# Where cache units lie in SBUF, how they are cut into loads, and a PSUM bank for the last output group, in a decode kernel that streams 282 MB

## The chip, the cores and the metric

One core of one Trainium2 chip. The metric is the device time of one execution in microseconds (us), as the median of several runs.

## The reference, cut to what matters

Four tokens (B = 4) go through a layer norm, then through an attention over a cache and through a small gated MLP, and the two results are added to the input.

```python
q = (xn @ wq).reshape(4, 1, 32, 128).transpose(0, 2, 1, 3)      # wq 640 x 4096
scores = einsum('bhqd,bhkd->bhqk', q, k_cache) * 128 ** -0.5     # k_cache 4 x 32 x 4096 x 128
p = softmax(scores)
o = einsum('bhqk,bhkd->bhqd', p, v_cache)                        # v_cache 4 x 32 x 4096 x 128
attention = o.transpose(0, 2, 1, 3).reshape(4, 1, 4096) @ wo     # wo 4096 x 640
# beside it: z = gelu(xn @ w_in), layer norm of one half, gate, @ w_out
return x + attention + mlp
```

All is bf16. K and V together are 268 MB, and each byte is used once. So this is a kernel that streams.

## The kernel before: the parts concerned

The heads are taken in 4 groups of 8, and a *unit* is one batch entry of one group: 128 partitions x 64 KB = 8.4 MB. There are 16 K units and 16 V units. The kernel's buffer in SBUF (the on-chip memory that loads land in) has five slots of half a unit, so a unit lies in two neighbouring slots.

```python
SL = T * Dh // 2                          # half a unit: 32 KB a partition
kv = const.tile([P, 5 * SL], BF16)        # five slots
# order of the loads, all on one queue: K0 K1 K2 K3 V0 K4 V1 K5 ... V11 K15 V12 V13 V14 V15
place = {("k", 0): 3, ("k", 1): 0, ("k", 2): 2, ("k", 3): 0}     # first of the two slots
for u in range(B, NU):
    place[("k", u)] = 1 if u % 2 == 0 else 0
for u in range(NU):
    place[("v", u)] = 3
place[("v", NU - 3)] = 1
place[("v", NU - 1)] = 0
# where a unit's load is cut (in tokens); a unit without an entry is one transfer
cuts = {("k", u): (0, T // 2, T) for u in range(NU) if u < B or u % B == B - 1}
cuts[("v", NU - 1)] = (0, 128, 192, 240, T)
first = {u: u % 2 for u in range(B, NU) if ("k", u) not in cuts}  # the half transposed first
```

wq lies in slots 0 and 1 at the start, w_in and w_out in slot 2. For each K unit VectorE makes 8 transposes (in blocks of 32 x 32, each element an f32 that holds two bf16), and TensorE multiplies each with the query. After four K units comes the softmax of the group, then the V units of the group are multiplied. A load waits until the last reader of its slots is done.

```python
nc.vector.transpose(kT[...], kw)                     # 8 of these per K unit
nc.tensor.matmul(S_ps[32 * q:32 * q + 32, e], ...)   # 8 per transpose
...
for w in range(NW):                                  # V: 64 matmuls, tokens in order
    nc.tensor.matmul(O_ps[32 * q:32 * q + 32], lhsT=Zb[b % 2][:, w], rhs=vv[:, w * 4 * Dh:(w + 1) * 4 * Dh], ...)
```

The tail: the output projection of all groups, the MLP and the residual collect in one bank of PSUM (the memory that TensorE's results go to), even rows of wo in partitions 0 to 63, odd ones in 64 to 127, and the halves are added at the end. The last group of wo loads in four pieces.

```python
emit_proj(NG - 1, range(0, HG // 2))
nc.vector.tensor_copy(out=o_1[:], in_=proj[64:128, 0:NO2])
emit_proj(NG - 1, range(HG // 2, HG))                 # all in partitions 0 to 63
nc.vector.tensor_tensor(out=o_bf[:], in0=proj[0:64, 0:NO2], in1=o_1[:], op=ALU.add)
# o_bf goes out on two queues
```

## Time and profile before

| what | before |
|---|---|
| median of the runs | 666.28 us, later 666.24 with 6 runs |
| span of the profiled run | 664.3 us |
| bytes read | 282.25 MB, 425 GB/s over the span |
| share of the load queue's packets in 16 engines' span | 98.7% |
| VectorE, TensorE busy | 54%, 45% |
| from the landing of the last wo piece (660.31) to the issue of the output (661.83) | 1.53 us |

In a timeline line the columns are start, length, engine, line of the kernel, operation, and in brackets the idle time ahead and what ended it. In a window line they are the window, its length, busy time and count of PE, PEld, DVE, ACT and POOL, then granted clock (of TensorE, as a share of full speed), DMA share and GB/s. The share books a packet's whole time at its start, so with packets of 2.4 us a window of 2 us can read above 1.

### The profile page before, as it was taken

What the parts mean: (1) busy time and instruction counts of PE and PEld (TensorE: products, weight loads), DVE (VectorE), ACT (ScalarE), POOL (GpSimd) and SP (SyncE); (2) the same over time, 40 slices, a digit from 0 to 9 for tenths busy, and PEclk for the clock granted to TensorE, in tenths of its full rate; (3) what the DMA queues carried; (4) which work ended last, traced back from release to release, by engine and by line L of the source; (5) the groups of instructions that cost most, each with busy time, mean ns of one, the idle gap of its engine ahead of it and who ended that gap; (6) DMA issues with size and microseconds to landing.
All of it is one profiled execution on the core that took longest, in us unless ns stands there. A gap on an engine that the chain in (4) does not pass through costs nothing.

```text
span 664.3 us, 5584 instructions
## 1 busy us (share of the span) xinstructions
PE 300.6 (45%) x2366; PEld 110.9 (17%) x2366; DVE 359.9 (54%) x340; ACT 82.6 (12%) x169; POOL 6.2 (1%) x24
## 2 busy tenths in 40 slices
PE   0566656336072556225436075533507154623154
PEld 0321212112021122001112022111202012211021
DVE  5388997456190849509155286745528084940002
ACT  0300000710100000530200000070100000062200
POOL 0000000000000000000000000000000000000000
PEclk9767876568576587677758576766957768767785
DMA  8999999999999999999999999999999999999995
GB/s 370 427 440 427 424 439 438 439 438 435 435 418 439 427 417 460 422 439 426 423 442 439 430 412 451 434 426 442 431 426 427 434 439 416 461 435 407 425 416 238
DMA packets 7669, 282.61 MB, mean 425 GB/s; under 512 B 872, under 2 KB 1244, under 8 KB 1756
## 3 DMA queue, kind: packets, MB, share of 16 engines
q1 hardware_dynamic: 7628, 282.25, 98.7%
q8 instruction: 18, 0.29, 0.2%
q14 instruction: 7, 0.06, 0.0%
q10 hardware_dynamic: 16, 0.01, 0.0%
HBM read 282.25 MB, written 0.01 MB: 425 GB/s over the span
## 4 chain that ended last, share of the span: by engine, by line
DMA 75%; issue 10%; DVE 10%; PE 3%; ACT 1%; SPq 0%; DVEq 0%; ACTq 0%
DMA kv<-in_A_k_cache_dram 64%; DVE kT L352 9%; DMA kv<-in_A_v_cache_dram 5%; DMA kv<-in_A_wo_dram 3%; DMA kv<-in_A_wq_dram 2%; PE O L434 2%; PE q L247 1%; DVE xd L417 0%; DVE kv L255 0%; ACT Zb L398 0%; PE proj L475 0%; ACT kv L255 0%; ACT p L406 0%; PE misc L278 0%; DVE pT L410 0%
## 5 line engine op out<-in xcount | busy, mean ns | idle before, releaser
L352 DVE STREAM_TRANSPOSE kT<-kv 128x2048 f32<-128x2048 f32 x128 | 283.4, 2277 | 127.4 <-DMA kv<-in_A_k_cache_dram 127.4
L363 PE MATMUL S<-kT,QZ 128*32 128x512 bf16 x1024 | 197.8, 522 | 227.1 <-DVE kT L352 227.1
L363 PEld LDWEIGHTS <-QZ 128*32 128x32 bf16 x1024 | 62.5, 114 | 356.8 <-issue 340.1
L434 PE MATMUL O<-kv,Zb 128*32 128x512 bf16 x1024 | 72.5, 444 | 61.3 <-ACT Zb L398 30.2
L441 DVE TENSOR_SCALAR R<-O,Mk 128x128 f32<-128x128 f32 x16 | 5.6, 351 | 126.4 <-PE O L434 126.4
L398 ACT ACTIVATE Zb<-xd,MkE 32x256 bf16<-32x256 bf16 x112 | 51.4, 498 | 111.7 <-PE O L434 110.3
L406 ACT ACTIVATE p<-S,negmax 128x512 bf16<-128x512 f32 x8 | 5.4, 683 | 395.1 <-DVE negmax L384 395.1
L434 PEld LDWEIGHTS <-Zb 128*32 128x32 bf16 x1024 | 31.9, 109 | 100.8 <-issue 54.5
L451 PE MATMUL misc<-R,SelR 128*32 128x128 f32 x32 | 6.6, 290 | 26.0 <-DVE R L443 26.0
L417 ACT COPY xd<-pT 32x256 bf16<-32x256 bf16 x28 | 17.2, 613 | 5.7 <-DVE pT L410 5.2
L443 DVE SCALAR_TENSOR_TENSOR R<-O,Mk,R 128x128 f32<-128x128 f32 x48 | 16.9, 351 | 1.7
L417 DVE COPY xd<-pT 32x256 bf16<-32x256 bf16 x36 | 13.1, 364 | 0.6
L339 POOL COPY QZ<-q 32x32 bf16<-32x32 bf16 x16 | 5.1, 320 | 422.6 <-PE S L363 395.3
L410 DVE STREAM_TRANSPOSE pT<-p 128x1024 bf16<-128x1024 bf16 x4 | 5.0, 1245 | 6.3 <-ACT p L406 6.3
L370 DVE TENSOR_REDUCE m<-S 128x2 f32<-128x1024 f32 x4 | 4.9, 1224 | 6.4 <-PE S L363 6.4
L451 PEld LDWEIGHTS misc<-R,SelR 128*32 128x32 f32 x32 | 2.3, 109 | 33.6 <-DVE R L443 24.8
L255 DVE CAST kv<-q 128x512 bf16<-128x512 f32 x4 | 2.5, 682 | 9.8 <-PE q L247 9.8
L475 PE MATMUL proj<-kv,oT 128*4 128x320 bf16 x64 | 6.3, 430 | 2.4 <-DMA kv<-in_A_wo_dram 1.8
L247 PE MATMUL q<-kv,xnT 128*32 128x512 bf16 x40 | 4.5, 629 | 5.5 <-DMA kv<-in_A_wq_dram 5.5
L454 DVE SCALAR_TENSOR_TENSOR om<-misc,rinv,MkH 32x1024 bf16<-32x1024 f32 x4 | 5.1, 1272 | 2.2 <-PE misc L451 2.2
L422 PE MATMUL misc<-rowsum,SelPe 128*32 128x1 f32 x16 | 2.1, 202 | 9.0 <-ACT p L406 9.0
L375 PE MATMUL misc<-dg,ones_f 128*128 128x256 f32 x8 | 2.7, 416 | 7.6 <-DVE dg L372 7.6
(94 smaller groups left out, 62.4 us busy)
## 6 DMA issues: line engine op xcount, KB each, us to landing
kv<-in_A_k_cache_dram SPq DMA_DIRECT2D x14, 4096.0 KB, 34.7
kv<-in_A_wq_dram SPq DMA_DIRECT2D x1, 5120.0 KB
kv<-in_A_v_cache_dram SPq DMA_DIRECT2D x1, 4096.0 KB, 40.2
kv<-in_A_wo_dram SPq DMA_DIRECT2D x3, 1280.0 KB, 19.2
kv<-in_B_w_in_dram SPq DMA_DIRECT2D x1, 2160.0 KB
kv<-in_A_v_cache_dram SPq DMA_DIRECT2D x1, 2048.0 KB
kv<-in_A_v_cache_dram SPq DMA_DIRECT2D x1, 1536.0 KB
kv<-in_B_w_out_dram SPq DMA_DIRECT2D x1, 960.0 KB, 22.6
```

The lines of the kernel that those rows point to most:

```text
L247: nc.tensor.matmul(q4_ps[32 * j:32 * j + 32, hf * 512:hf * 512 + 512], lhsT=xnT[:, c, :], rhs=wq[:, c, n0:n0 + 512], start=(c == 0), stop= ...
L339: nc.gpsimd.tensor_copy(out=QZ[r0:r0 + 32, :, :, :, 8 + 8 * hp], in_=q3[r0:r0 + 32, :, NE * hp:NE * hp + NE, g * B:g * B + B].rearrange("p ...
L352: nc.vector.transpose(kT[:].rearrange("p (t r) -> p t r", r=32), kw)
L363: nc.tensor.matmul(S_ps[32 * q:32 * q + 32, e], lhsT=QZ[:, b, 2 * kh + w, e, w0:w0 + 32], rhs=kb[:, i, :, e, :, w], start=(b == 0 and k < ...
L398: nc.scalar.activation(out=dst, in_=src, func=ACT.Copy, scale=mk)
L406: nc.scalar.activation(out=p_bf[:, :, e, :], in_=S_ps[:, e], func=ACT.Exp, bias=negmax[:, e:e + 1], scale=scale, accum_out=rowsum[:, e:e + 1])
L417: op(out=xd[32 * hp:32 * hp + 32, :, q, :], in_=pT[32 * q:32 * q + 32, :, hp, :].rearrange("p t x -> p x t"))
L434: nc.tensor.matmul(O_ps[32 * q:32 * q + 32, :, :], lhsT=Zb[b % 2][:, w].rearrange("p h c -> p (h c)"), rhs=vv[:, w * 4 * Dh:(w + 1) * 4 * ...
L441: nc.vector.tensor_scalar(out=R, in0=O_ps[:, 0, :], scalar1=Mk4[:, 0:1], scalar2=None, op0=ALU.mult)
L443: nc.vector.scalar_tensor_tensor(out=R, in0=O_ps[:, c, :], scalar=Mk4[:, c:c + 1], in1=R, op0=ALU.mult, op1=ALU.add)
L451: nc.tensor.matmul(oh[:], lhsT=SelR[:, b].rearrange("p h b -> p (h b)"), rhs=state["R"][:, b, :], start=(b == 0), stop=(b == B - 1))
L475: nc.tensor.matmul(proj[r0:r0 + B, 0:NO2], lhsT=oT[:, c, :], rhs=wo_t[g][:, c, hf * NO2:(hf + 1) * NO2], start=False, stop=(g == NG - 1 an ...
```

## The change

The intent: with the slots dealt the other way round, K0 to K2 can each load as one transfer without V0 waiting for all of K2; K3 lies in slots 4 and 0, which are not neighbours, and keeps its two halves. V15 loads in two pieces and not four. The last wo group gets a PSUM bank of its own, so that its matmuls need not wait until the old bank is read.

```diff
-    place = {("k", 0): 3, ("k", 1): 0, ("k", 2): 2, ("k", 3): 0}
+    place = {("k", 0): (3, 4), ("k", 1): (0, 1), ("k", 2): (2, 3), ("k", 3): (4, 0)}
     for u in range(B, NU):
-        place[("k", u)] = 1 if u % 2 == 0 else 0
+        place[("k", u)] = (3, 4) if u % 2 == 0 else (2, 3)
     for u in range(NU):
-        place[("v", u)] = 3
-    place[("v", NU - 3)] = 1
-    place[("v", NU - 1)] = 0
-    cuts = {("k", u): (0, T // 2, T) for u in range(NU) if u < B or u % B == B - 1}
-    cuts[("v", NU - 1)] = (0, 128, 192, 240, T)
+        place[("v", u)] = (0, 1)
+    place[("v", 0)] = (1, 2)
+    place[("v", NU - 3)] = (2, 3)
+    place[("v", NU - 1)] = (3, 4)
+    cuts = {("k", u): (0, T // 2, T) for u in range(NU) if u % B == B - 1}
+    cuts[("v", NU - 1)] = (0, 192, T)
 ... (cut: addressing of a unit by its two slots; wo groups in slots 4, 0, 1, 2 and not 2, 4, 3, 2)
-                nc.sync.dma_start(out=x_res[0:32:4, :], in_=x_flat.rearrange("b (h n) -> (b h) n", h=NH))
+                for r0, r1 in ((0, 3), (3, 2 * B)):
+                    nc.sync.dma_start(out=x_res[4 * r0:4 * r1:4, :], in_=x_rows[r0:r1])
 ...
-    emit_proj(NG - 1, range(0, HG // 2))
-    nc.vector.tensor_copy(out=o_1[:], in_=proj[64:128, 0:NO2])
-    emit_proj(NG - 1, range(HG // 2, HG))
+    nc.vector.tensor_copy(out=o_1[:], in_=proj[0:64, 0:NO2])
+    nc.vector.tensor_tensor(out=o_1[:], in0=proj[64:128, 0:NO2], in1=o_1[:], op=ALU.add)
+    last = ps_l.tile([64, NO2], F32)
+    for c in range(HG):                    # c == 0 starts the bank, with 32 columns
+        for hf in range(NH):
+            nc.tensor.matmul(last[32 * hf:...], lhsT=..., rhs=wo_t[NG - 1][:, c, hf * NO2:(hf + 1) * NO2],
+                             start=(c == 0), stop=(c == HG - 1))
-    nc.vector.tensor_tensor(out=o_bf[:], in0=proj[0:64, 0:NO2], in1=o_1[:], op=ALU.add)
+    nc.vector.tensor_tensor(out=o_bf[:], in0=last[:], in1=o_1[:], op=ALU.add)
```

More of the change, by code (lines that the diff above doesn't have):

```diff
@@ L72 @@
     ps_j = ctx.enter_context(tc.tile_pool(name="ps_j", bufs=1, space=bass.MemoryType.PSUM))
+    ps_l = ctx.enter_context(tc.tile_pool(name="ps_l", bufs=1, space=bass.MemoryType.PSUM))
     misc_ctr = [0]
@@ L120, with unit @@
             seq.append(("k", u + B))
-    place = {("k", 0): 3, ("k", 1): 0, ("k", 2): 2, ("k", 3): 0}
+    place = {("k", 0): (3, 4), ("k", 1): (0, 1), ("k", 2): (2, 3), ("k", 3): (4, 0)}
     for u in range(B, NU):
-        place[("k", u)] = 1 if u % 2 == 0 else 0
+        place[("k", u)] = (3, 4) if u % 2 == 0 else (2, 3)
     for u in range(NU):
-        place[("v", u)] = 3
-    place[("v", NU - 3)] = 1
-    place[("v", NU - 1)] = 0
-    cuts = {("k", u): (0, T // 2, T) for u in range(NU) if u < B or u % B == B - 1}
-    cuts[("v", NU - 1)] = (0, 128, 192, 240, T)
-    first = {u: u % 2 for u in range(B, NU) if ("k", u) not in cuts}
-    def unit(item):
-        return at_slot(place[item], 2 * SL)
+        place[("v", u)] = (0, 1)
[4 more added lines that the diff above has]
+    cuts[("v", NU - 1)] = (0, 192, T)
+    first = {u: u % 2 for u in range(B, NU) if ("k", u) not in cuts}
+    def unit(item, t0, t1):
+        s0, s1 = place[item]
+        assert s1 == s0 + 1 or t1 <= T // 2 or t0 >= T // 2
+        if t0 >= T // 2:
+            return at_slot(s1, (t1 - t0) * Dh, t0 * Dh - SL)
+        return at_slot(s0, (t1 - t0) * Dh, t0 * Dh)
     def load_unit(item):
@@ L138, in load_unit @@
         cache = A_k_cache if key == "k" else A_v_cache
-        dst = unit(item)
         src = cache[b, g * HG:(g + 1) * HG].rearrange("e (m t) d -> (e m) (t d)", t=T)
@@ L142, in load_unit @@
         for t0, t1 in zip(c[:-1], c[1:]):
-            nc.sync.dma_start(out=dst[:, t0 * Dh:t1 * Dh], in_=src[:, t0 * Dh:t1 * Dh])
+            nc.sync.dma_start(out=unit(item, t0, t1), in_=src[:, t0 * Dh:t1 * Dh])
     wo_q = A_wo.rearrange("(g p c) n -> g p c n", p=P, c=HG)
-    wo_t = [at_slot((2, 4, 3, 2)[g], HG * NOUT).rearrange("p (c n) -> p c n", c=HG) for g in range(NG)]
+    wo_t = [at_slot((4, 0, 1, 2)[g], HG * NOUT).rearrange("p (c n) -> p c n", c=HG) for g in range(NG)]
     def load_wo(g, c_cuts=(0, HG)):
@@ L349, in emit_K @@
         qp, kh = k // 2 % 2, k % 2
-        kw = unit(("k", u)).bitcast(F32).rearrange("p (x t w) -> p x t w", w=KW, t=2 * TC)[:, 2 * hh + qp, :, 32 * kh:32 * kh + 32]
+        t0 = 2 * TC * (2 * hh + qp)
+        kw = unit(("k", u), t0, t0 + 2 * TC).bitcast(F32).rearrange("p (t w) -> p t w", w=KW)[:, :, 32 * kh:32 * kh + 32]
         kT = ktpool.tile([P, 2 * TC * 32], F32, tag="kT", name="kT")
@@ L430, in emit_V @@
         O_ps = ps_o.tile([P, 4, Dh], F32, tag="O", name="O")
-        vv = unit(("v", v))
+        vv = unit(("v", v), 0, T)
         for w in range(NW):
@@ L471, in emit_proj @@
             for hf in range(NH):
-                odd = c % 2 == 1 and not (g == NG - 1 and c >= HG // 2)
-                r0 = 64 * odd + 32 * hf
+                r0 = 64 * (c % 2) + 32 * hf
                 nc.tensor.matmul(proj[r0:r0 + B, 0:NO2], lhsT=oT[:, c, :],
                                  rhs=wo_t[g][:, c, hf * NO2:(hf + 1) * NO2],
-                                 start=False, stop=(g == NG - 1 and c in (HG // 2 - 1, HG - 1)))
+                                 start=False, stop=(g == NG - 2 and c >= HG - 2))
     fill_qz(0)
@@ L483 @@
             if u == NU - 2 and key == "v":
-                nc.sync.dma_start(out=x_res[0:32:4, :], in_=x_flat.rearrange("b (h n) -> (b h) n", h=NH))
+                x_rows = x_flat.rearrange("b (h n) -> (b h) n", h=NH)
+                for r0, r1 in ((0, 3), (3, 2 * B)):
+                    nc.sync.dma_start(out=x_res[4 * r0:4 * r1:4, :], in_=x_rows[r0:r1])
             load_unit(seq[i + 1])
@@ L518 @@
     emit_proj(NG - 2, range(4, HG))
-    emit_proj(NG - 1, range(0, HG // 2))
     o_1 = const.tile([64, NO2], F32)
-    nc.vector.tensor_copy(out=o_1[:], in_=proj[64:128, 0:NO2])
-    emit_proj(NG - 1, range(HG // 2, HG))
+    nc.vector.tensor_copy(out=o_1[:], in_=proj[0:64, 0:NO2])
+    nc.vector.tensor_tensor(out=o_1[:], in0=proj[64:128, 0:NO2], in1=o_1[:], op=ALU.add)
+    last = ps_l.tile([64, NO2], F32)
+    oT = state[("oT", NG - 1)]
+    for c in range(HG):
+        lhsT = oT[:].rearrange("p c b -> p (c b)") if c == 0 else oT[:, c, :]
+        for hf in range(NH):
+            nc.tensor.matmul(last[32 * hf:32 * hf + (32 if c == 0 else B), :], lhsT=lhsT,
+                             rhs=wo_t[NG - 1][:, c, hf * NO2:(hf + 1) * NO2], start=(c == 0), stop=(c == HG - 1))
     o_bf = const.tile([64, NO2], BF16)
-    nc.vector.tensor_tensor(out=o_bf[:], in0=proj[0:64, 0:NO2], in1=o_1[:], op=ALU.add)
+    nc.vector.tensor_tensor(out=o_bf[:], in0=last[:], in1=o_1[:], op=ALU.add)
     nc.sync.dma_start(out=out_flat[:, 0:NO2], in_=o_bf[0:B, :])
```

## The prediction

> **What bounds the kernel now**
>
> I read four views in this order: the page's slices and queues, the busy time by window, the chain of work that ended last, and the timelines of the load queue and of VectorE around the first softmax.
>
> The page first: which resource is full?
>
> ```profile
> DMA  8999999999999999999999999999999999999995
> q1 hardware_dynamic: 7628, 282.25, 98.7%
> HBM read 282.25 MB, written 0.01 MB: 425 GB/s over the span
> ```
>
> The DMA digit is 9 in every slice but the first and the last, and the packets of the load queue fill 98.7% of the 16 engines' span of 664.3 us. TensorE (45%) and VectorE (54%) have room. So I ask only where the DMA engines are not full. The windows say so (columns: window and length, busy us and instructions of PE, PEld, DVE, ACT, POOL, then granted clock, DMA share, GB/s):
>
> ```profile
> 2.00:20.00 18.00, 3.83 (x41) 1.88 (x45) 8.31 (x36) 0.91 (x2) 0.00 (x0) 1.00 0.94 399
> 100.00:140.00 40.00, 17.32 (x120) 5.94 (x117) 20.34 (x29) 14.97 (x31) 1.27 (x4) 0.67 1.02 442
> 600.00:655.00 55.00, 20.35 (x226) 8.14 (x218) 6.66 (x17) 7.21 (x16) 0.00 (x0) 0.70 0.99 423
> 655.00:664.00 9.00, 4.10 (x48) 1.69 (x40) 1.39 (x4) 0.00 (x0) 0.00 (x0) 0.50 0.26 104
> ```
>
> From 20 to 655 us the share is about 1; only the last 9 us (0.26) are not transfer. The whole change can therefore win in three places: bytes or time per byte in the full stretch, a hole in it (there is none in the windows of before, so a change can only make one), and the tail. The chain of waits shows the tail:
>
> ```profile
> 637.05 21.66 DMA kv<-in_A_wo_dram
> 658.71 0.04 issue
> 658.75 0.73 PE proj L475 x8
> ...
> 659.51 0.50 DVE o L521
> ...
> 660.05 1.25 PE proj L475 x8
> ...
> 661.32 0.48 DVE o_bf L525
> ```
>
> The first piece of the last wo group lands at 658.71. Then 8 matmuls, a copy of half of the projection bank, 8 more matmuls and the final add follow each other; the output goes out at 661.83 and the program ends at 664.3. By the semaphore records the other three pieces of that group land at 659.49, 659.91 and 660.31, so the last 8 matmuls (660.05 to 661.30) start before the last piece is there.
>
> Last, the place where loads depend most tightly on compute, the first softmax (first the load queue, then VectorE and TensorE, then a link of the chain):
>
> ```profile
> 92.19 0.33 SPq L143 DMA_DIRECT2D kv<-in_A_v_cache_dram  x1
> 111.63 0.33 SPq L143 DMA_DIRECT2D kv<-in_A_k_cache_dram  x1
> 132.25 0.33 SPq L143 DMA_DIRECT2D kv<-in_A_v_cache_dram  x1
> ```
>
> ```profile
> 83.28 8.89 DVE L352 STREAM_TRANSPOSE kT<-kv 128x2048 f32<-128x2048 f32 x4 [0.83 <-DMA kv<-in_A_k_cache_dram]
> 92.99 8.89 DVE L352 STREAM_TRANSPOSE kT<-kv 128x2048 f32<-128x2048 f32 x4 [0.82 <-DMA kv<-in_A_k_cache_dram]
> 102.71 8.89 DVE L352 STREAM_TRANSPOSE kT<-kv 128x2048 f32<-128x2048 f32 x4 [0.84 <-DMA kv<-in_A_k_cache_dram]
> ```
>
> ```profile
> 126.46 5.74 PE L434 MATMUL O<-kv,Zb 128*32 128x512 bf16 x64 [7.55 <-ACT Zb L398]
> ```
>
> ```profile
> 111.63 29.66 DMA kv<-in_A_k_cache_dram
> ```
>
> The four first K units come in halves, and VectorE transposes each half (8.89 us) inside the 9.7 us that the next half takes to land. It is done with K3 at 111.6. The second V unit is issued at 132.25, when the product of V0 (126.46 plus 5.74) has freed its slots. The unit ahead of it in the queue, K4, lands at 111.63 + 29.66 = 141.29 (its 16 engines finish between 139.39 and 141.29). So this issue is 7 to 9 us ahead of an empty queue.
>
> **What the Trainium skill says**
>
> "DMA: Bandwidth & Descriptors", Specifications, gives a fabric ceiling of 435 GB/s for one core's 16 engines, and about 358 GB/s as the HBM limit per core. The trace goes with the first: 423 to 442 GB/s in the full windows. There is no rate left to win.
>
> Same page, "Why a DMA increments its semaphore by 16 and not by 1": each engine counts up when its share has landed, and the wait is for all. The trace agrees: the shares of K4 land over 1.90 us, those of the last wo piece over 4.72 us (655.58 to 660.31). It also says that 8 rows run on 8 engines, 3 on 3 and 5 on 5, the lowest-numbered; so the split of x_res moves two or three packets of 640 B (about 32 ns each here) off engines 5 to 7. No view of this trace tells the engines apart.
>
> Same page, "Latency and other measured facts": about 600 ns from issue to first byte. Here the first load is issued at 0.73 and its first packets start at 1.75, the last of the 16 engines near 2.9: 1.0 to 2.2 us, and I use these.
>
> "TensorE: Matmul & The Clock Gate", "Wait — 56ns, not 53.3ns?": start to start is N / 1.2 GHz while the array is cold, so 267 ns for 320 columns. The trace agrees: granted clock 0.50 at the end, and the projection matmuls start in groups 267 ns apart, four at a time where four 32-column groups are used, two at a time where two are.
>
> **The change part by part**
>
> *Slots.* Mirrored, V in (0,1), even K in (3,4), odd K in (2,3). The shared slot of two neighbouring K units is again the one transposed first, so from the fifth unit on every load waits for the same product as before. Worth 0. The bytes are the same.
>
> *K0 to K2 whole.* Saved per unit: two halves land 9.711 us apart each (34.452, 44.163, 53.876 by the semaphore records), 19.42 together; a whole unit takes 19.35 (121.943 to 141.292). That is 0.07 us, three times: 0.2 us of queue time.
>
> *V15 in two pieces, not four.* The four land at 640.98, 645.88, 649.72 and 650.98 after V14 at 631.26: 19.72 us. One cut costs about 0.07 over 19.35, so 19.42. Saved: 0.3 us.
>
> *The cost of whole units.* VectorE starts on K0 at 44.2 and not 34.5. Eight transposes take 17.7 us (K4: 141.315 to 158.976; 2.19 a step), under the 19.4 us between units. K0 is done at 61.8, K1 (landing 63.5) at 81.2. K2 lands at 82.9; its 8 and the 8 of K3, whose halves have landed by 102.4, run without a gap: 16 x 2.19 + 0.1 = 35.2, so to 118.2 and not 111.6. That is 6.6 us later. Everything from there to V0 is compute (softmax, spreading, 64 matmuls), 20.6 us, so V1 is issued at 138.8 and not 132.25. K4 now drains at 139.2 to 141.1. With 1.0 to 2.2 us from issue to packet, V1's packets start at 139.8 to 141.0. The engines that are done first wait about 0.6 us, the last one about nothing. As the end is set by the last engine, I charge 0.2 us.
>
> The other early loads are not tight: K2 needs K0's first half (44.2 + 8.9 = 53.1) against a drain at 63.5; V0 needs K2's first half (92.0) against 102.4; K4 needs K3's first half (109.4) against 121.7.
>
> *The tail.* The last group gets a bank, so its 16 matmuls no longer stand behind the copy; copy and an added add (0.50 + 0.48) lie beside them. But all 16 go to two column groups: 8 pairs x 0.267 = 2.1 us from 658.75, the last pair starting near 660.6 and ending at 661.04, against 661.28 before. So 0.24 us, no more: the wait of 0.5 us goes, and half of it comes back as serial pairs. V15's last piece is 64 tokens and not 16: 16 matmuls (four groups of 0.427) and not 4, so oT comes some 0.7 us later, near 656.9, still ahead of 658.7.
>
> Sum: -0.2 - 0.3 + 0.2 - 0.24 = about -0.5 us, so 666.28 becomes 665.7 us.
>
> **The rivals**
>
> *The queue runs dry before V1.* If the softmax stretch takes 2 us more than I think (VectorE not keeping the 2.19 us step over 16 transposes, for instance), each engine idles about 2 us near 140 and nothing later wins it back, as the rest is full: near 667.7. Against it: the step is steady in all K units of this trace. For it: my margin is only about 1 us. It cannot be large: with a late start of 5 us the time is 671, still within 1%.
>
> *The tail follows the landing.* If the clock is granted in full at the end, the pairs take 0.133 us and the last one waits for the landing at 660.31: done near 660.7, 0.3 us better, 665.4.
>
> *The spread of the engines changes.* The last wo piece ends 4.7 us apart on fast and slow engines. If the new cuts, the split of x_res or a pause near 140 bring the engines together by 1 us, the end comes up to 1 us earlier: 664.7. Nothing in the profile says which engine is slow, so this widens the range only.
>
> **Range and chances**
>
> Predicted 665.7 us. The good rivals reach 664.7, the dry queue of 1 to 2 us 667: range 664.6 to 667.2. A gain of 2% would be 13.3 us, more than all that isn't transfer; a loss of 2% would need a hole of 13 us, and the tight load is late by 1 at most. Faster 0.01, same 0.98, slower 0.01.
>
> **What would show each step right or wrong**
>
> The queue's packets at about 98.7% of the span again; K0 to K2 landing some 19.35 us apart; VectorE busy without a gap from 83 to 118 us; the V1 issue near 139 and a DMA share a little under 1 around 140 us; from K5 on the same issue intervals; a last group of 16 matmuls that no DVE wait cuts, ending 0.6 us before the end of before's; the copy and the add ahead of it. Wrong if the V1 issue comes after 140, if another load is issued into an empty queue, or if the share of the packets moves by more than half a per cent.

## The result, and the profile after

The changed kernel takes 665.38 us (665.20 to 665.74, 6 runs) against 666.24 us (666.10 to 666.30, 6 runs). The ratio is 0.9988, 95% interval 0.9975 to 1.0001. A ratio here and below is the mean time of one kernel's fast runs over that of the other's of the same rounds, so it is not quite the ratio of the medians. Every run of the changed kernel lies below every run of before, by about 0.86 us in the medians.

The page of the changed kernel (slices and load queue):

```profile
DMA  9999999999999999999999999999999999999996
q1 hardware_dynamic: 6908, 282.25, 98.8%
HBM read 282.25 MB, written 0.01 MB: 425 GB/s over the span
```

The bound is the same: the DMA engines are full, with 720 packets fewer. VectorE at the start (timeline of the changed kernel):

```profile
44.26 17.66 DVE L360 STREAM_TRANSPOSE kT<-kv 128x2048 f32<-128x2048 f32 x8 [11.33 <-DMA kv<-in_A_k_cache_dram]
63.78 17.66 DVE L360 STREAM_TRANSPOSE kT<-kv 128x2048 f32<-128x2048 f32 x8 [1.86 <-DMA kv<-in_A_k_cache_dram]
83.13 35.20 DVE L360 STREAM_TRANSPOSE kT<-kv 128x2048 f32<-128x2048 f32 x16 [1.69 <-DMA kv<-in_A_k_cache_dram]
```

K0, K1 and then K2 with K3 are each transposed in one go; VectorE is done at 118.33 and not 111.6, as expected. TensorE and the load queue after that (timelines of the changed kernel):

```profile
118.39 1.15 PE L371 MATMUL S<-kT,QZ 128*32 128x512 bf16 x8 [1.07 <-DVE kT L360]
...
132.46 5.47 PE L442 MATMUL O<-kv,Zb 128*32 128x512 bf16 x64 [7.56 <-ACT Zb L406]
```

```profile
136.11 0.33 SPq L150 DMA_DIRECT2D kv<-in_A_v_cache_dram  x1
150.21 0.33 SPq L150 DMA_DIRECT2D kv<-in_A_k_cache_dram  x1
164.28 0.33 SPq L150 DMA_DIRECT2D kv<-in_A_v_cache_dram  x1
```

V1 is issued at 136.11, while V0's product is still running (it ends at 132.46 + 5.47 = 137.93). The issues of K5 and V2 (150.21, 164.28) are within 0.1 us of those of before; later ones up to V14 differ by up to 1.2 us in both directions (V4 at 241.70 against 242.84), but each of them is issued at least 5.3 us before the first engine has done the load ahead of it. That the queue does not run dry at the late V1 is seen in the windows of the changed kernel:

```profile
138.00:140.00 2.00, 0.35 (x2) 0.23 (x3) 1.39 (x4) 1.95 (x5) 0.00 (x0) 1.00 0.94 401
140.00:142.00 2.00, 0.02 (x1) 0.00 (x0) 0.71 (x1) 1.65 (x4) 0.00 (x0) 1.00 1.15 492
```

The tail, from the chain of waits and the timeline of VectorE:

```profile
635.86 22.43 DMA kv<-in_A_wo_dram
658.29 0.04 issue
658.34 2.25 PE last L537 x16
660.59 0.02 issue
660.61 0.48 DVE o_bf L541
```

```profile
657.56 0.48 DVE L529 COPY o<-proj 64x320 f32<-64x320 f32 x1 [0.97 <-PE proj L481]
658.08 0.49 DVE L530 TENSOR_TENSOR o<-proj,o 64x320 f32<-64x320 f32 x1
```

Sixteen matmuls run without a break, copy and add lie ahead of and beside them, and one add follows. By the semaphore records the last wo piece lands at 659.93 (before: 660.31) and the output is issued at 661.12 (661.83). So of the 0.71 us by which the output comes earlier in these two traces, 0.38 comes from the loads and 0.34 from the tail. These are one trace each: in a second trace of the changed kernel (`after_again`, below) the last piece lands at 660.09 and the output is issued at 661.38, so 0.22 and 0.23.

### The profile page after: what moved, and what is told of

Its sections match the earlier page's. It is cut to its first block, busy times and chain, and to the rows that moved or that the text cites. A ratio compares the mean times of both kernels' runs of the same rounds, so it can differ in the third digit from the quotient of the medians.

```text
span 663.5 us, 5584 instructions
## 1 busy us (share of the span) xinstructions
PE 298.7 (45%) x2366; PEld 111.7 (17%) x2366; DVE 359.9 (54%) x341; ACT 82.6 (12%) x169; POOL 6.2 (1%) x24
## 3 DMA queue, kind: packets, MB, share of 16 engines
q1 hardware_dynamic: 6908, 282.25, 98.8%
## 4 chain that ended last, share of the span: by engine, by line
DMA 73%; DVE 12%; issue 11%; PE 2%; ACT 1%; SPq 0%; DVEq 0%; ACTq 0%
DMA kv<-in_A_k_cache_dram 65%; DVE kT L360 11%; DMA kv<-in_A_v_cache_dram 4%; DMA kv<-in_A_wo_dram 3%; PE O L442 2%; DVE xd L425 0%; PE last L537 0%; ACT Zb L406 0%; ACT p L414 0%; DVE pT L418 0%; DVE m L378 0%; PE misc L383 0%; PE S L371 0%; SPq L111 0%; ACT xd L425 0%
## 5 line engine op out<-in xcount | busy, mean ns | idle before, releaser
L371 PE MATMUL S<-kT,QZ 128*32 128x512 bf16 x1024 | 192.8, 511 | 230.4 <-DVE kT L360 230.4
L442 PE MATMUL O<-kv,Zb 128*32 128x512 bf16 x1024 | 76.3, 464 | 59.7 <-ACT Zb L406 30.2
```

The source lines that it names most:

```text
L371: nc.tensor.matmul(S_ps[32 * q:32 * q + 32, e], lhsT=QZ[:, b, 2 * kh + w, e, w0:w0 + 32], rhs=kb[:, i, :, e, :, w], start=(b == 0 and k < ...
L442: nc.tensor.matmul(O_ps[32 * q:32 * q + 32, :, :], lhsT=Zb[b % 2][:, w].rearrange("p h c -> p (h c)"), rhs=vv[:, w * 4 * Dh:(w + 1) * 4 * ...
```

## The experiments

### The parts alone

`tail_only` is the kernel before with the new tail; `slots_only` is the changed kernel with the old tail.

```diff
 # tail_only, against before
+    last = ps_l.tile([64, NO2], F32)        # and the new end, as in the change; slots and cuts as before
 # slots_only, against the changed kernel
-    last = ps_l.tile([64, NO2], F32)        # and the old end, as in before
```

> The kernel before with nothing but the new tail: last wo group in its own PSUM bank, copy and add of the other groups beside it. My theory: the loads are as before, the last matmul ends 0.25 to 0.35 us earlier than before relative to the landing of the last wo piece, so 666.24 becomes about 665.9 us. Rival (the whole gain of 0.86 us comes from the loads): 666.2. Rival (the whole gain comes from the tail): 665.4.

> The changed kernel with the tail of before: mirrored slots, K0 to K2 whole, V15 in two pieces, split x_res. My theory: last wo piece lands about 0.4 us before that of before, so about 665.8 us. Rival (all in the tail): 666.2. V1 issued near 136 us as in the changed kernel.

Measured: `tail_only` 665.72 us (665.48 to 666.00, 5 runs), `slots_only` 665.65 us (665.55 to 665.89, 5 runs), before 666.16 us (665.92 to 666.36, 9 runs). Ratios 0.9995 and 0.9993; both intervals contain 1, so the single parts are not clear of noise by the interval, but the medians lie 0.44 and 0.51 us below, and every run of `slots_only` and four of the five of `tail_only` lie below every run of before. Together that is 0.95, and the whole change measures 0.86. By the medians neither rival (all in the loads, all in the tail) fits: both parts count.

The tail part is larger than the 0.25 to 0.35 us expected. The one run that was profiled shows a possible reason (matmuls of the last group, and the window around the end, of `tail_only`):

```profile
658.66 1.98 PE L528 MATMUL last<-kv,oT 128*32 128x320 bf16 x16 [0.28 <-DMA kv<-in_A_wo_dram]
```

```profile
660.00:662.00 2.00, 0.64 (x8) 0.25 (x4) 0.48 (x1) 0.00 (x0) 0.00 (x0) 0.96 0.00 1
```

In this run the clock was granted nearly in full (0.96) for the last matmuls, so the pairs went faster and ended right behind the last landing (660.22); the output was issued 0.97 us after it, against 1.53 in before. In the changed kernel's profile the clock fell to half at 658.46 and it took 1.19 us.

The traces settle the size at half clock. From the landing of the first of the four last wo pieces to the issue of the output takes 3.12 to 3.13 us in the three traces with the old tail (before, `slots_only`, `whole_old_slots`) and 2.91 in the seven with the new tail in which the granted clock was half all through it. So the new tail itself is worth 0.22 us. In the other three, in which the clock was full for part of it, it takes 2.58 to 2.83 us (`tail_only`, `balanced`, the changed kernel); that extra belongs to the clock of that run. All three old tails ran at half clock, so what they would take at full clock isn't shown. How the clock stood in the four runs of `tail_only` that were not profiled isn't known.

One profile is one run: in that of `slots_only` the last landing (660.26) is only 0.05 us earlier than in before, though its median is 0.5 us lower. Tenths of the whole time are read from the medians of five runs, one profile only says where to look.

### Whole units without the mirrored slots, and mirrored slots with halves

```diff
 # whole_old_slots, against before
-    cuts = {("k", u): (0, T // 2, T) for u in range(NU) if u < B or u % B == B - 1}
+    cuts = {("k", u): (0, T // 2, T) for u in range(NU) if u % B == B - 1}
 # halves_new_slots, against the changed kernel: the same line the other way
```

> The kernel before with only the cuts of K0 to K2 taken away, slots as before. Then V0 goes to slots 3 and 4 and waits for all of K2 (done near 101 us), while the queue ahead of it drains between 100.4 and 102.4. My theory: V0 issued near 101, its packets from about 102 to 103, a hole of 0.5 to 1.5 us, so 666.6 to 667.5 us. Rival (the mirrored order is not needed for whole units): no hole, 666.0.

> The changed kernel with K0 to K2 cut in halves again. My theory: cutting costs 0.07 us a unit, so 0.2 us over the changed kernel: about 665.6 us; V1 issue back near 130 to 132 us. Rival (the whole units cost as much as they save, because of the later V1): 665.4, no difference or faster.

Measured: `whole_old_slots` 666.67 us (666.54 to 668.97, 5 runs), ratio to before 1.0015, interval 1.0003 to 1.0028: slower by the interval, and its mean holds one long run (668.97); the medians differ by 0.5 us. `halves_new_slots` 665.69 us (665.67 to 665.89, 5 runs), ratio to before 0.9994, against 0.9988 of the changed kernel. The load queue of `whole_old_slots`, and the same window of it and of before:

```profile
100.74 0.33 SPq L143 DMA_DIRECT2D kv<-in_A_v_cache_dram  x1
118.28 0.33 SPq L143 DMA_DIRECT2D kv<-in_A_k_cache_dram  x1
139.20 0.33 SPq L143 DMA_DIRECT2D kv<-in_A_v_cache_dram  x1
```

```profile
102.00:104.00 2.00, 1.70 (x10) 0.47 (x7) 2.00 (x2) 0.00 (x0) 0.00 (x0) 0.50 0.43 164
```

```profile
102.00:104.00 2.00, 1.71 (x8) 0.41 (x8) 1.29 (x1) 0.00 (x0) 0.00 (x0) 0.64 1.06 459
```

V0 goes to slots 3 and 4, must wait for the last transposes of K2 and is issued at 100.74, when the queue has 0 to 1.5 us of work left. Its first packets start at 101.7 to 102.5, the DMA share falls to 0.43 in a window where before has 1.06, and the kernel loses 0.5 us although it has three transfers fewer. So the mirrored order does what it is for: in slots 1 and 2 V0 needs only the first half of K2 and is issued at 92.05.

One thing I hadn't asked for: after the hole the 16 engines run closer together. In before the first and the last engine finish the last wo piece 4.7 us apart, here 3.2 (657.90 to 661.10), so K4 lands 1.75 us later than in before, and the last piece only 0.8.

`halves_new_slots` issues V1 at 129.10 and still is slower than the changed kernel, by 0.0006 of 666 = 0.4 us in the ratios. Its last landing (660.13) doesn't decide it: the two traces of the changed kernel have 659.93 and 660.09. What a trace shows without that scatter is the time between two landings in it: from K0 to K2 it is 38.69 to 38.72 us in all nine traces with whole units, and 38.85 in three of the four with halves (38.99 in before). That is 0.07 us a unit, so 0.2 us for the three. No cost of the later V1 shows.

### What a cut costs

```diff
 # cut_all, against the changed kernel: every K and V unit that is one transfer becomes two halves
+    every = {(key, u): (0, T // 2, T) for key in ("k", "v") for u in range(NU)}
+    every.update(cuts)
-        c = cuts.get(item, (0, T))
+        c = every.get(item, (0, T))
 # v15_four, against the changed kernel
-    cuts[("v", NU - 1)] = (0, 192, T)
+    cuts[("v", NU - 1)] = (0, 128, 192, 240, T)
```

> The changed kernel with every K and V unit loaded in two halves: 25 cuts more than the changed kernel (12 K units and V15 have nothing or other cuts counted out). My theory: 0.07 us of queue time a cut, so the last load lands about 1.8 us later: 667.2 us. Rival (a cut costs nothing, the gain of whole units has another cause): 665.4. Rival (a cut costs 0.13 us, as the packet times alone say): 668.6.

> The changed kernel with V15 loaded in four pieces (128, 64, 48, 16 tokens) as before. My theory: two cuts more cost 0.2 to 0.3 us of queue time, so 0.2 to 0.3 us over the changed kernel of this call, about 665.6 us. Rival (the pieces cost nothing): no difference.

I had miscounted for `cut_all`: 12 K units and 15 V units are cut anew, so 27 cuts and not 25. Measured: 667.54 us (667.33 to 667.66, 4 runs), ratio to before 1.0023 against 0.9988, so 0.0035 x 666 = 2.3 us, or 0.09 us a cut. In its trace the last wo piece lands at 661.82, 1.89 us after that of the changed kernel: 0.07 us a cut (0.06 against the trace of `after_again`). The rival with no cost is out, and so is the one of 0.13 us from the lengths of the packets alone. `v15_four` measured 665.57 us (665.48 to 665.66) against 665.31 us (665.22 to 665.54) of the changed kernel: 0.26 us for two cuts, within what was expected. The traces say less: from the landing of V14 to that of V15 takes 19.42 to 19.44 us in the eight traces with V15 in two pieces (all but `balanced`) and 19.57 to 19.60 in three of the four with four pieces. That is 0.15 us for two cuts; the 19.72 of before, which the prediction used, is the highest of all.

> The changed kernel once more, as the yardstick of this call: 0.9988 of the time before, about 665.3 us.

This yardstick run gave the ratio 0.9988 a second time, 665.31 us against 666.18.

### How much room the later V1 has

```diff
 # late2 and late5, against the changed kernel: useless work on VectorE behind K3
+            if u == B - 1:
+                kw = unit(("k", u), T - 2 * TC, T)...[:, :, 32:64]
+                for _ in range(2):                     # 5 in late5
+                    kT = ktpool.tile([P, 2 * TC * 32], F32, tag="kT", name="kT")
+                    nc.vector.transpose(kT[:].rearrange("p (t r) -> p t r", r=32), kw)
```

> The changed kernel with two useless transposes (2.2 us each, and a wait for TensorE) on VectorE ahead of the first softmax. The V1 issue moves from 136.1 to about 141 to 142 us, the queue ahead of it drains between 139.1 and 141.3, and a first packet comes 1.0 to 2.2 us after an issue. My theory (the margin is about 3 us, past it each us is lost for good): 666.5 to 667.5 us, and a DMA share under 0.7 near 141 to 143 us. Rival (a late V1 is hidden or won back by the end): 665.4.

> The same with five useless transposes: V1 issued near 148 to 149 us. My theory: some 8 us past the margin, all but 1 us of it lost: 672 to 674 us. Rival (hidden or won back): under 667.

Measured: `late2` 666.19 us (666.06 to 666.29, 4 runs), ratio to before 1.0002; `late5` 672.80 us (672.73 to 673.12), ratio 1.0103. Against the changed kernel that is 0.0014 x 666 = 0.9 us and 0.0115 x 666 = 7.7 us. The issues of V1, and a window of `late5` while it waits:

```profile
139.26 0.33 SPq L150 DMA_DIRECT2D kv<-in_A_v_cache_dram  x1
```

```profile
146.09 0.33 SPq L150 DMA_DIRECT2D kv<-in_A_v_cache_dram  x1
```

```profile
140.00:142.00 2.00, 0.00 (x0) 0.00 (x0) 0.53 (x2) 1.90 (x5) 0.00 (x0) 0.50 0.00 0
```

V1 came 3.15 and 9.98 us later than in the changed kernel (136.11), less late than I had put it for either, in part because VectorE's wait of 1.24 us for the last query product ahead of the softmax is gone: that product now runs beside the useless transposes. So `late2` is 0.3 us below the range that I had given, and `late5` within it. Its landing moved from 160.47 to 161.09 and 167.88, so by 0.62 and 7.41 us. Both give nearly the same margin: 3.15 - 0.62 = 2.5 and 9.98 - 7.41 = 2.6 us (2.0 and 2.3 if V1's landing is counted from K4's in the same trace). Past it each microsecond is lost, and the end shows it again (last landing 660.86 and 667.44 against 659.93: 0.93 and 7.51). The rival "hidden or won back" is out. With the queue empty, the first packets of V1 in `late5` start 0.96 to 2.1 us after its issue, much as the prediction had taken them from the start of the program.

### The split of x_res

```diff
 # xres_whole, against the changed kernel
-                for r0, r1 in ((0, 3), (3, 2 * B)):
+                for r0, r1 in ((0, 2 * B),):
```

> The changed kernel with x_res loaded in one transfer of 8 rows. My theory: 640 B packets of 0.03 us on engines 5 to 7 that are not the last ones; no difference, 665.3 us. Rival (the split decides which engine is last): 665.6 us or more.

Measured: 665.57 us, with 665.41 to 665.58 in four runs and 666.99 in the fifth, against 665.22 to 665.54 of the changed kernel. The ranges overlap and the one long run is the one whose profile was kept. The trace of that long run shows that the split isn't what made it long: its engines land V13, the load just ahead of x_res in the queue, 5.5 us apart already (4.0 in the changed kernel). Whether the split is worth 0.2 us or nothing stays open.

### A try at the spread of the engines

The last wo piece ends 4.8 us apart on the 16 engines of the changed kernel (655.11 to 659.93). I followed the packets of each engine through the packet records: the next packet of an engine mostly starts within 4 ns of the end of the one before, so this can be done, with some doubt where two engines coincide. All 18 packets of 16 KB of instruction fetches lie on the same 8 engines, two or three on each, about 1.1 us apiece, and most packets behind one take about another 0.5 us. The engines without fetches finish the load queue at 654.6 to 656.0 (one, with other small loads, at 658.5), those with two at 657.6 to 658.0, the two with three at 659.3 and 659.5. I tried to take load off them:

```diff
 # balanced, against the changed kernel: the last 64 tokens of V14 as 96 + 8 + 8 + 3 + 3 + 3 + 3 + 3 + 1 rows
+    cuts[("v", NU - 2)] = (0, T - 64, T)
+    ROWS = (0, 96, 104, 112, 115, 118, 121, 124, 127, 128)
-            nc.sync.dma_start(out=unit(item, t0, t1), in_=src[:, t0 * Dh:t1 * Dh])
+            rows = ROWS if (item, t0) == (("v", NU - 2), T - 64) else (0, P)
+            for r0, r1 in zip(rows[:-1], rows[1:]):
+                nc.sync.dma_start(out=unit(item, t0, t1)[r0:r1], in_=src[r0:r1, t0 * Dh:t1 * Dh])
```

> The changed kernel with the last 64 tokens of V14 loaded not as one transfer of 128 rows but as 96 rows (6 on each of 16 engines), twice 8 rows (one on each of engines 0 to 7), five times 3 rows and 1 row (on the lowest 3 engines and the first). In the traces of before and after, 8 engines carry all 18 instruction fetches and end up to 4.7 us after the others; the x_res packets say that engines 0 to 2 carry none. My theory: two rows of 16 KB (0.61 us each) less on the slow engines bring the last landing from 659.9 to about 658.7, limited by one engine that carries other small loads: about 664.4 us. Rival (the late engines are not the ones relieved): 665.4 or up to 668.

Measured: 675.71 us (675.21 to 675.90, 4 runs), ratio to before 1.0144. Much worse, and the windows of this kernel show where:

```profile
610.00:620.00 10.00, 6.76 (x68) 2.67 (x67) 1.40 (x4) 2.61 (x6) 0.00 (x0) 0.67 0.98 419
620.00:630.00 10.00, 0.00 (x0) 0.00 (x0) 0.00 (x0) 0.99 (x3) 0.00 (x0) 0.50 0.97 213
630.00:640.00 10.00, 5.12 (x48) 2.01 (x48) 0.00 (x0) 0.00 (x0) 0.00 (x0) 0.67 0.69 184
```

From 620 to 630 the engines are as busy as ever (0.97) and move half as much. The packets of 16 KB of these row-wise transfers took 1.28 us in the median, where the packets of the same size in a transfer of 128 rows took 0.61 in the changed kernel. From 630 to 640 the queue also runs dry: the loads use eight semaphores (the counters that tell of a landing) in turn, an issue waits until the load that had its semaphore before has landed (the issues at 631.75 and 637.75 follow landings at 631.74 and 637.74), and V15 is issued only at 638.09 (616.13 in the changed kernel). The rows were not alone in being slow: the last packets of V14's other part, which has 128 rows, took up to 4.6 us in this stretch, and 1.82 before it. Whether the slow packets or the dry queue cost more was not separated, and the idea of giving the late engines less isn't refuted by this; this way of doing it is.

No version here beats the changed kernel.

## Why the prediction was right

**The bound: right.** The load queue's packets fill 98.8% of the span, and a change of 2% was never within reach.

**Slots worth nothing from K5 on: right.** The issues at 150.21 and 164.28 are those of before, and no later one comes nearer than 5.3 us to an empty queue.

**K0 to K2 whole, 0.2 us: right. V15 in two pieces, 0.3 us: right in kind, about double.** From K0's to K2's landing the traces give 0.07 us a unit, and `cut_all` gives 0.06 to 0.09 us a cut over 27 cuts. For V15 the traces give 0.15 us; the prediction took the 19.72 us of the one trace that it had, where three others with the same pieces have 19.57 to 19.60. The medians of `v15_four` differ by 0.26 us, so the prediction isn't refuted there. The size of a cut came from landing times of whole and halved units. The mean packet lengths alone would have said nearly twice as much, and `cut_all` rules that out.

**VectorE done at 118.2: right (118.33).**

**V1 issued at 138.8: wrong (136.11; 136.67 in `after_again`).** The prediction carried over the whole 20.6 us from the last transpose to the V1 issue of before. It overlooked what the mirrored order does there: V0 lies in slots 1 and 2, V1 in 0 and 1, so V1 waits for the first 32 matmuls of V0 only. They take 3.65 us (132.46 to 136.11), where before waited for all 64 (5.79, 126.46 to 132.25). That is 2.1 us; another 0.7 us is the last query product, at full clock in this run (1.15 us and not 1.89; 1.60 in `after_again`), and that part is luck. So the 0.2 us charged for a late V1 became nothing. The mechanism itself was sized well: with a margin of 2.5 us, an issue at 138.8 would have been about 0.2 us too late.

**The tail, 0.24 us: right at half clock.** The estimate had all 16 matmuls at half clock, and the seven traces in which that holds give 0.22. In the changed kernel's own trace it holds from 658.46 on only, and the tail is 0.34 us shorter. In `tail_only` the clock rose to full at 660.16, and the rival "the tail follows the landing" comes near that run. How often a run gets that clock isn't known.

**The rivals.** The queue did not run dry in the changed kernel; it did in `whole_old_slots`, `late2` and `late5`, at the cost that the rival gave per microsecond. The spread of the engines didn't change (4.8 us against 4.7), so the rival that made it 1 us better doesn't describe this run.

The sum was 0.5 us and 0.86 was measured. With what the traces show, the sum is 0.2 (K0 to K2) + 0.15 (V15) + 0.22 (tail) and nothing for V1, so about 0.57. That the forecast came this close is in part luck: the charge for V1 that was not due and the double size for V15 nearly cancelled. The remaining 0.3 us is not attributed. A full clock in the tail of some runs and the split of x_res (0 to 0.2 us) are candidates; no run here separates them.

## What to carry to other kernels

Where the DMA engines are full from start to end, a change of layout can only save what the transfers cost in themselves (here 0.07 us a cut) and in the tail, and it can lose much more by making one issue late: so compute, for each load, the issue time against the time at which the queue ahead drains, and add the 1 to 2 us to the first packet. Look up which part of the earlier reader a load really waits for; half a unit of overlap was worth 2 us of margin here. Placement and cutting belong together: the same whole units that gain in the mirrored slots lose in the old ones.

## What the Trainium skill lacked or had wrong

- "DMA: Bandwidth & Descriptors", Latency and other measured facts: the first byte of an HWDGE transfer is put at about 600 ns. With an empty queue the first packets of an 8.4 MB load started 0.96 us after the start of the issuing instruction on the first engine and 2.1 us on the last (`late5`). That instruction takes 0.33 us, so from its end the first engine has 0.63 us, which agrees; that the last of 16 engines starts 1.2 us after the first is not told.
- The same page, Specifications: the row with the HBM limit per core, about 358 GB/s, did not bind this program on a single core: it moved 425 GB/s over the span, near the fabric ceiling that the page gives too. The page's own single-core measurement (425 GB/s for 16 MB) agrees with the trace.
- The same page, Rules for kernel authors, has no cost for cutting one large transfer in two while the queue is full: 0.07 us for 8.4 MB (`cut_all`, 27 cuts, 1.89 us).
- "Runtime: NRT & Kernel Launch", Instruction fetch mechanics, has the blocks of 16 KiB, but not on which DMA engines they run or what they cost loads beside them: here 18 packets of 16 KB fell on 8 of the 16 engines, about 1.1 us each, and these engines ended up to 4.8 us behind the first. This was followed through the packet records, not read off a view.
- "DMA: Bandwidth & Descriptors", The descriptor swizzle, describes transfers of 128 partitions; that packets can take twice as long when transfers of 96, 8 and 3 rows follow each other is not told: packets of 16 KB took 1.28 us and not 0.61 (`balanced`). "SBUF — State Buffer", Door 1: The DMA port swizzle, says that bandwidth depends on how many ports the partitions reach, which may be part of the cause; but rows 0 to 95 reach all 16 by that page's table, and no run here shows it.
